# A search's new order for a fused attention and mixing kernel: pieces of its 32-row value products set apart

## The chip, the cores and the metric

The program runs on one core of one Trainium2 chip. The metric is the device time of one execution in microseconds (us), lower is better. The core's engines work side by side, each through its own list of instructions: TensorE (PE in the profile; its weight loads are PEld), VectorE (DVE), ScalarE (ACT), GpSimd (POOL), and SyncE (SP), which here only issues DMAs. They meet at semaphores.

## What is computed

The reference, cut to what matters; there are 8 batches, 8 heads, 576 positions and 64 numbers per head, all in fp32:

```python
scores = matmul(q, k.T) / sqrt(64)
scores = where(scores >= scores.max(-1) - tau, scores, -1e9)
attn = exp(scores - scores.max(-1));  attn = attn / (attn.sum(-1) + 1e-9)
x = matmul(attn, v)                                # heads side by side: (8, 576, 512)
theta = x @ w_theta
y = w_tok_r @ (x * cos(theta)) + w_tok_i @ (x * sin(theta))
u = x + y
out = u + maximum(u @ w_ch, 0)
```

## The kernel before

The 64 heads are worked in 32 pairs. For each pair five *units* of score products run on TensorE (line 761, 12 or 6 matmuls each). VectorE takes the scores out of PSUM with their largest value (782), ScalarE makes the exponentials (815), VectorE masks and sums them (822). Then the weights of the attention are turned round, in one of two ways. In 12 pairs TensorE does it with transposes (855) and the value product runs with 64 rows (920). In the other 20 pairs VectorE turns blocks of 32 by 32 (837, 839), and the value product runs with 32 rows and 64 columns of the array, eight such products side by side (891): 144 fp32 matmuls of 144 columns in the program, which become 288 passes in the trace, each with a weight load of its own. These are the *small value products* of this text. All of a pair's value product goes into PSUM banks 0 to 3, and ScalarE copies it out at its end (904, 907). After every fourth pair a batch is complete and its mixture follows: angles and the last product on TensorE (1021), sines on ScalarE (1117 to 1124), products with x on GpSimd or VectorE (1139), transposes of z (1164) and the token product (1209). The mixture of one batch is spread among the attention of the next.

A pair's small value products are cut into three *pieces*, each one step of the plan with 48 matmuls of the program:

```python
parts = AT["parts"]                                # 3
for i in range(parts):
    c0, c1 = 18 * i // parts, 18 * (i + 1) // parts
    pe((c1 - c0) * w / 600 + 0.05, lambda c0=c0, c1=c1: products(c0, c1),
       key + A("vs", n) * i, (a, v), (ps,), 32 * (c1 - c0), mode="w", hold=[x])
```

The code first makes a list of 4617 steps, each for one engine, with what it reads and writes. Nothing is scheduled when the kernel is built: the table `ORDER` holds, as differences, the numbers of the steps in the order in which they are emitted, and the table `PLACES` holds the buffer of each class that a step's tile takes. Both come from an offline search over a plan with costs; the search is not part of the file. `Plan.run` walks the table:

```python
n = 0
for word in ORDER.split():
    step, times = (word + "*1").split("*")[:2]
    for _ in range(int(times)):
        n += int(step)
        self.ops[n].fn()
```

Each engine gets its own steps in that order and works them strictly one after another.

Of the kernel before, what the change touches and what calls it, by code (L numbers as in the profile page):

```python
# [142 lines left out]
    "176 3 -9 3 75 -71 -176 177 2 -153 144 10 -9 79 -251 183 -169 160 -134 135 -122 131 146 -145 2 -1 3 8 -9 -186 "  # L143
    "188 59 -246 195 -5 -189 191 4 -8 10 -5 4 11 -19 -187 197 1 -197 22 185 -204 185 -187 205 -197 202 -13 21 27 -2 "
    "-43 8 38 -27 -21 4 -193 211 2 25 -40 17 8 -11 -220 325 -125 8 -206 2 198 -156 164 195 -372 14 127 58 -19 -15 "
    "-164 181 -212 219 26 -239 225 -229 228 -9 -10 -3 -189 301 -74 -20 -4 -9 -168 164 15 23 -229 209 22 -17 27 64 -2 "
    "-98 10 91 -99 51 210 -238 13 -10 26 -42 90 -91 26 -228 220 30 -4 -28 -14 43 -16 10 11 122 -141 18 -21 24 -279 "
    "273 -16 223 -479 280 -3 -19 21 9 -22 15 -278 260 -16 42 -283 258 3 -18 35 6 -40 -2 38 -25 26 -286 394 -113 -270 "
    "290 -300 281 -10 12 -281 258 41 93 -383 232 -240 299 -290 278 -285 312 -28 -276 279 -58 57 -34 140 -104 -49 155 "
    "-385 304 -20 -4 -36 -241 279 102 -79 -16 -288 30 350 -98 24 -1 -16 27 -32 -283 306 1 -16 -289 287 43 -40 173 "  # L150
    "-148 -38 571 -534 -26 43 -326 332 -21 -10 13 8 -321 311 3 12 -304 -21 332 -309 -1 309 5 -3 1 -23 -309 335 7 -53 "
    "30 14 -13 -317 299 -2 44 -41 537 -526 29 -3 -24 -15 -292 306 41 -11 -346 342 -24 -5 -302 445 -424 305 -23 44 "
    "-59 26 133 -119 -1 -326 -10 455 -108 -336 1 336 -3 28 -330 800 -505 -317 -8 333 -345 449 -428 -7 309 -26 153 "
    "-77 -16 -335 429 -438 361 -344 -7 1 362 -355 -16 341 -301 321 -18 -6 -320 -30 348 28 -345 -8 877 -527 -332 -9 "
    "-7 326 -327 9 289 27 52 -55 -312 1 8 316 -2 -331 297 62 -38 55 -16 -26 -318 -6 367 -26 -19 46 -366 349 -321 309 "
    "33 -18 -346 10 344 11 -4 -17 -333 355 -373 19 333 25 -3 1 -367 -6 352 -343 -2 855 -488 -31 40 -53 14 -326 343 "
    "15 -16 -3 -16 -333 350 -330 353 -26 -336 21 339 3 -40 -312 -20 375 119 -148 11 13 4 -372 -1 18 -9 2 317 58 -11 "
    "-373 18 309 -319 332 36 9 -375 30 334 -355 345 425 -386 -17 -366 -9 780 -769 353 -363 329 444 -764 366 399 -381 "
    "-380 28 -40 364 -12 422 -764 3 378 -376 352 535 -533 6 -364 393 -388 437 -83 23 -51 52 27 -43 -13 3 37 372 -355 "
    "-43 -3 30 -389 349 474 -417 -28 338 -356 47 -406 1 9 390 -10 -388 9 705 -327 -377 366 13 -368 -10 872 -168 -693 "  # L160
    "383 -404 22 694 -705 -10 725 -337 -13 22 19 -27 -388 716 -706 2 -10 9 -10 396 -18 -2 -356 359 -377 372 350 -347 "
    "15 -2 -15 -354 367 5 -2 334 -711 10 -2 -10 714 -14 -689 -8 722 -348 327 -309 -382 689 -701 396 -5 -377 711 79 "
    "-100 -315 -376 695 -2 -309 -7 -375 383 4 324 -19 -304 -11 317 -305 312 -311 338 -344 -6 334 -327 -5 22 297 30 "
    "61 -398 298 10 -304 389 -394 2 337 2 55 -384 36 263 -308 344 -343 391 -449 60 1 309 24 -26 34 -5 57 -88 10 -5 "
    "-304 302 149 -448 297 -305 343 -26 -308 332 -335 4 -3 345 -37 -314 317 18 17 5 -16 -331 343 -20 -322 343 -327 "
    "288 43 -330 331 -330 315 -312 -20 349 -6 -322 -20 347 7 -24 20 -333 315 3 -317 -17 350 -303 301 174 -167 -354 3 "
    "350 -352 4 -3 4 356 -50 9 -317 39 291 -327 356 -28 -310 19 -34 331 -301 -14 15 396 -428 10 23 399 -404 8 14 -32 "
    "-19 12 312 -294 340 65 -422 18 91 -100 -8 416 -307 -100 101 -104 323 -319 410 80 -395 252 60 -368 -24 60 215 "
    "-214 -75 16 79 716 -735 246 -245 19 -100 19 63 247 -27 -214 1 238 -306 62 -89 341 -251 -62 9 54 -80 316 -231 "
    "-65 79 -81 68 -85 22 77 -13 -68 19 43 7 260 -321 -6 18 292 -230 -73 -26 87 -67 7 61 721 -706 -81 58 9 -51 -8 17 "  # L170
    "57 -76 11 20 46 -72 73 -77 78 214 -213 1 -69 20 -29 33 26 -29 283 -281 -1 261 -210 -48 49 238 -22 -263 56 243 "
    "-256 214 -200 -9 -49 -24 74 9 -14 -79 13 72 -48 43 14 -92 84 -77 27 59 2 -1 -9 206 -255 60 5 -15 11 5 218 -217 "
    "230 -324 288 37 -20 21 -16 137 -369 234 -197 187 17 -314 111 197 -196 187 -303 319 -314 309 -312 303 21 -320 "
    "105 -33 16 219 -201 -17 -88 89 1 -89 109 198 -217 20 202 -207 -103 109 -63 -47 90 217 5 -220 216 10 2 -272 -46 "
    "319 -2 3 2 -211 184 -294 90 230 7 -32 -293 74 246 -321 322 -245 13 194 44 -209 -28 236 5 -212 1 202 6 1 6 -12 "
    "-214 223 -241 39 -38 244 -194 -21 -28 237 7 1 13 -17 -212 217 -229 242 -258 17 242 -241 221 -220 252 -41 16 "
    "-226 243 10 -244 306 -314 251 -12 -238 317 -338 -9 293 55 -338 287 -277 325 -314 241 -3 29 46 -299 254 -261 244 "
    "3 -239 303 -302 683 -447 3 -238 18 -108 81 1 -19 273 -305 52 243 -235 -7 8 -7 14 1 212 -217 224 -226 244 -243 "
    "24 -22 246 -245 220 21 -237 217 15 13 -244 232 -14 9 18 -244 240 5 -17 -16 34 11 -28 18 -241 207 395 -350 -31 "
    "-220 196 56 -10 -248 9 253 -13 21 -11 1 -13 -246 239 429 -406 -9 -4 -240 241 20 -19 352 -597 254 -6 -244 242 "  # L180
    "-245 264 -6 7 -261 277 -287 265 7 -271 605 -340 -253 276 53 -75 340 -593 296 -17 -278 273 -49 36 36 -49 346 "
    "-592 260 21 15 291 -340 50 -22 -18 54 277 -306 -281 273 381 -397 25 -281 1 273 22 3 257 -554 281 -7 24 -11 16 "
    "252 -256 -19 20 -18 65 -64 18 412 -157 2 -254 -2 258 -276 273 2 5 -278 2 1 19 -13 271 -256 1 254 -269 13 -33 "
    "291 7 -269 -30 37 340 -339 -7 17 325 -86 -248 254 82 -333 258 -251 -9 45 -42 251 80 -59 -271 -53 310 -291 285 "
    "-245 247 -256 398 -386 233 -232 248 -257 10 261 -238 -27 5 17 -27 6 236 -231 17 1 -17 261 -240 238 -241 4 -3 "
    "219 25 -230 -32 33 -11 222 -221 4 -26 265 -27 6 -211 234 -266 26 -22 261 -264 2 275 -4 -272 20 -17 32 280 -60 "
    "22 -20 -232 -21 274 -247 248 -243 -30 35 224 196 -188 -236 -11 290 -50 -7 -254 37 338 -112 -1 7 6 -248 -24 19 "
    "16 -5 231 -213 -49 32 18 218 -101 -141 25 404 -403 137 -162 45 203 -629 368 59 180 -216 207 -191 21 190 -210 5 "
# [1197 lines left out]
```

## Time and profile before

| | |
|---|---|
| Time, median of 3 runs | 952.08 us (949.31 to 953.31) |
| Time of the profiled execution | 950.14 us |
| Its span, first to last instruction | 948.3 us |
| PE busy | 904.9 us (95%) |
| DVE busy | 796.5 us (84%) |
| ACT busy | 634.1 us (67%) |
| POOL busy | 342.8 us (36%) |
| Small value products (L891), PE busy, and idle just before them | 105.9 us, 12.9 us |

The profiled execution is 1.94 us shorter than the median of the runs. Busy time of PE is the union of its matmuls' times; a matmul's end is modelled and overlaps the next one's start, so a short wait of PE can lie unseen inside busy time.

### The profile page before, as it was taken

Reading aid. Unit: us, or ns where it says so; the run is one execution under the profiler, and the core shown is the slowest. Engines: PE = TensorE matmul, PEld = TensorE weight load, DVE = VectorE, ACT = ScalarE, POOL = GpSimd, SP = SyncE. Lnnn points to the kernel's source line nnn. Section 1 sums busy time; section 2 is a strip of 40 time slices with the busy share of each in tenths; the row PEclk is TensorE's granted clock in tenths of the full one; section 3 lists DMA queues with packets and bytes.
Section 4 is the critical chain, followed back from the end, with each engine's and each line's share of the span. In section 5 each row is a group of like instructions: output and inputs, shape, how many; then the busy total and the mean of one; then the engine's idle time right before and its main releaser. Section 6 shows DMA issues by size and latency. Waiting matters only on the chain.

```text
span 948.3 us, 30033 instructions
## 1 busy us (share of the span) xinstructions
PE 904.9 (95%) x12532; PEld 801.8 (85%) x12532; DVE 796.5 (84%) x1838; ACT 634.1 (67%) x1296; POOL 342.8 (36%) x390
## 2 busy tenths in 40 slices
PE   6889999999999999999899999999999999999998
PEld 5667788898898889888798988898898988899798
DVE  7999899979988988889798897879998798986342
ACT  7899997458945777467764767548784578635650
POOL 2234453125624345234432533432442353404110
PEclk9999999999999999999999999999999999999999
DMA  6366253435322353325403453044533153222322
GB/s 219 125 195 199 85 184 125 142 123 192 122 86 92 116 178 120 127 78 179 147 37 104 136 192 112 4 172 122 192 99 112 55 196 123 70 97 98 114 70 73
DMA packets 59288, 118.80 MB, mean 125 GB/s; under 512 B 19441, under 2 KB 28561, under 8 KB 56593
## 3 DMA queue, kind: packets, MB, share of 16 engines
q1 hardware_dynamic: 59008, 116.89, 37.2%
q8 instruction: 98, 1.61, 0.7%
q14 instruction: 38, 0.30, 0.1%
q10 hardware_dynamic: 144, 0.00, 0.0%
HBM read 103.09 MB, written 13.78 MB: 123 GB/s over the span
## 4 chain that ended last, share of the span: by engine, by line
PE 60%; DVE 22%; ACT 10%; issue 5%; POOL 2%; DMA 0%; SPq 0%; DVEq 0%; ACTq 0%; POOLq 0%
PE banks_ps__66 L1209 19%; PE banks_ps__66 L1021 12%; PE banks_ps__66 L761 10%; PE banks_ps__66 L891 9%; DVE sc L782 6%; DVE s L822 6%; PE banks_ps__66 L855 4%; DVE a L837 4%; PE banks_ps__66 L1164 3%; PE banks_ps__66 L920 2%; ACT s L815 2%; POOL z L1139 1%; DVE xl L539 1%; DVE z L1089 1%; ACT L1117 1%
## 5 line engine op out<-in xcount | busy, mean ns | idle before, releaser
L815 ACT ACTIVATE s<-sc,nm 128x576 f32<-128x576 f32 x288 | 219.5, 777 | 73.0 <-DVE sc L782 57.3
L822 DVE SCALAR_TENSOR_TENSOR s<-sc,nm,s 128x576 f32<-128x576 f32 x288 | 249.7, 888 | 14.9 <-ACT s L815 7.9
L782 DVE TENSOR_SCALAR_CACHE_REDUCE sc<-banks_ps__66 128x576 f32<-128x576 f32 x261 | 188.3, 744 | 23.0 <-PE banks_ps__66 L761 21.7
L761 PE MATMUL banks_ps__66<-k,q 64*128 64x288 f32 (+1 forms) x1728 | 173.9, 313 | 12.9 <-DVE sc L782 7.9
L1021 PE MATMUL banks_ps__66<-xh,wm 128*128 128x288 f32 x1024 | 170.9, 304 | 2.2 <-issue 1.6
L761 PEld LDWEIGHTS banks_ps__66<-k,q 64*128 64x128 f32 (+1 forms) x1728 | 137.9, 189 | 39.8 <-issue 15.2
L1209 PE MATMUL banks_ps__66<-wt_h,zh 128*128 128x288 f32 x576 | 159.1, 303 | 1.3 <-ACT zh L1170 0.4
L1209 PE MATMUL banks_ps__66<-wt_l,zh 128*128 128x288 f32 x576 | 158.0, 299 | 0.0
L1021 PEld LDWEIGHTS banks_ps__66<-xh,wm 128*128 128x128 f32 x1024 | 144.8, 190 | 9.5 <-issue 6.2
L1139 POOL TENSOR_TENSOR z<-z,xT 128x288 f32<-128x288 f32 x112 | 98.7, 914 | 128.6 <-ACT z L1120 118.0
L837 DVE STREAM_TRANSPOSE a<-s 128x576 f32<-128x576 f32 x160 | 117.4, 757 | 20.6 <-PE banks_ps__66 L891 18.6
L539 POOL TENSOR_TENSOR xl<-xT,xh 128x288 fp32r<-128x288 f32 x78 | 75.3, 987 | 141.8 <-ACT xh L982 120.5
L891 PE MATMUL banks_ps__66<-a,v 32*64 32x144 f32 x5760 | 105.9, 286 | 12.9 <-issue 11.0
L1209 PEld LDWEIGHTS banks_ps__66<-wt_h,zh 128*128 128x128 f32 x576 | 106.8, 188 | 7.0 <-issue 4.1
L891 PEld LDWEIGHTS banks_ps__66<-a,v 32*64 32x64 f32 x5760 | 91.5, 130 | 23.5 <-issue 18.9
L1209 PEld LDWEIGHTS banks_ps__66<-wt_l,zh 128*128 128x128 f32 x576 | 107.3, 188 | 2.0 <-issue 1.9
L539 POOL TENSOR_TENSOR k<-rawk,k 128x288 fp32r<-128x288 f32 x62 | 57.9, 942 | 113.7 <-ACT k L722 78.1
L1209 PE MATMUL banks_ps__66<-wt_h,zl 128*128 128x288 f32 x576 | 98.7, 299 | 0.0
L539 POOL TENSOR_TENSOR q<-rawq,q 128x320 fp32r<-128x320 f32 x56 | 57.8, 1045 | 111.8 <-ACT q L708 111.8
L1021 PE MATMUL banks_ps__66<-xl,wm 128*128 128x288 f32 x512 | 92.6, 301 | 0.9 <-DVE xl L539 0.6
L1209 PEld LDWEIGHTS banks_ps__66<-wt_h,zl 128*128 128x128 f32 x576 | 82.8, 188 | 1.4 <-issue 1.2
L855 PE MATMUL banks_ps__66<-ident,s 128*128 128x128 f32 (+1 forms) x492 | 74.8, 284 | 3.1 <-DVE s L822 2.1
(84 smaller groups left out, 1275.0 us busy)
## 6 DMA issues: line engine op xcount, KB each, us to landing
wm<-wm_dram SPq DMA_DIRECT2D x64, 512.0 KB
v<-in_vp_dram SPq DMA_DIRECT2D x20, 1152.0 KB
rawq<-in_qT_dram SPq DMA_DIRECT2D x31, 320.0 KB
rawk<-in_kT_dram SPq DMA_DIRECT2D x31, 288.0 KB
out_dram<-xT SPq DMA_DIRECT2D x31, 288.0 KB
rb<-sums_dram SPq DMA_DIRECT2D x64, 128.0 KB
v<-in_vp_dram SPq DMA_DIRECT2D x12, 576.0 KB
z<-in_w_tok_dram SPq DMA_DIRECT2D x9, 576.0 KB
```

Of the source, the lines that this page charges most:

```text
L539: eng.tensor_tensor(out=out()[:, c0:c1], in0=in0()[:, c0:c1], in1=in1()[:, c0:c1], op=ALU.subtract)
L761: nc.tensor.matmul(ps()[:, 2 * j + h, :HS], q[a]()[r, i * P : (i + 1) * P], k[c]()[r, h * HS : (h + 1) * HS], start=(x == 0), stop=(x == 2),)
L782: lambda j=j, sc=sc, scaled=scaled: nc.vector.tensor_scalar(out=sc().rearrange("p (a b) -> p a b", a=2), in0=ps()[:, 2 * j : 2 * j + 2, :H ...
L815: lambda j=j, sc=sc, weights=weights: nc.scalar.activation(out=weights(), in_=keys(sc()), func=AF.Exp, bias=nm()[:, j : j + 1], scale=-1.0),
L822: lambda j=j, sc=sc, total=total, weights=weights: nc.vector.scalar_tensor_tensor(out=weights(), in0=keys(sc()), scalar=nm()[:, 2 + j : 3 ...
L837: nc.vector.transpose(out=a()[:, :, j, 32 * i : 32 * i + 32], in_=src.rearrange("p (c q) -> p c q", q=32))
L855: nc.tensor.transpose(out=tp()[: k1 - k0, c * P : (c + 1) * P], in_=flat()[:, k0:k1], identity=ident)
L891: nc.tensor.matmul(ps()[64 * h : 64 * h + 64, b, :w], v()[r, c, h, :], a()[r, c, h, :], start=(c == 0), stop=(c == 17))
L1021: nc.tensor.matmul(ps[h]()[:, :HS], wm()[:, a, c, :], parts[c][bb]()[:, h * HS : (h + 1) * HS], start=first and n == 0, stop=final and n = ...
L1139: eng.tensor_tensor(out=zi, in0=zi, in1=x[m]()[:, c0:c1], op=ALU.mult)
L1164: nc.tensor.transpose(out=tp()[:, i * P : (i + 1) * P], in_=z()[:, c : c + P], identity=ident)
L1209: nc.tensor.matmul(ps()[:, :HS], zz[c][lo]()[:, zz[c][2]], w[:, c, hs], start=(q + n == 0), stop=(q + n == len(work) - 1),)
```

## The change

Only `ORDER` differs: other numbers, one line more. The list of steps, their code, the buffers of `PLACES` and all cost numbers are the same, so every line below the table moves from L to L+1 (L891 is L892 in the new file), and every instruction runs the same work on the same tiles. On VectorE 701 of 1225 steps stand at another place in its list, on ScalarE 650 of 1170, on GpSimd 252 of 384 and among the DMA issues 193 of 292; the mean step there moves by 1.1 to 1.3 places and the furthest by 16. A line or two of the table:

```diff
 ORDER = (
-    "176 3 -9 3 75 -71 -176 177 2 -153 144 10 -9 79 -251 183 -169 160 -134 135 -122 131 146 -145 2 -1 3 8 -9 -186 "
...
+    "13 9 5 -4 16 -11 7 -3 4 -3 4 3 -2 3 2 -1 2 "
 )
```

The clearest difference is on TensorE. In the order before, 17 of the 20 pairs have two of their three pieces directly behind each other, 96 matmuls in a row (a *doubled piece*). In the rows below L1021 is the mixture's products of channels, L1164 the transposes of z, L946 a transpose of the row sums, L855 the transposes of attention weights and L1209 the token product; `xh` and `xl` are the two parts of an operand, `zh` and `zl` too. On TensorE before, all three pieces of the pair that stands at 457 to 468 us of the trace:

```order
L891 MATMUL banks_ps__66<-a,v 64x144 x48
L1021 MATMUL banks_ps__66<-xl,wm 128x288 x4
L1021 MATMUL banks_ps__66<-xh,wm 128x288 x8
L891 MATMUL banks_ps__66<-a,v 64x144 x96
L1164 MATMUL banks_ps__66<-ident,z 128x128 x4
```

The same pair after:

```order
L892 MATMUL banks_ps__66<-a,v 64x144 x48
L1022 MATMUL banks_ps__66<-xh,wm 128x288 x8
L1022 MATMUL banks_ps__66<-xl,wm 128x288 x4
L892 MATMUL banks_ps__66<-a,v 64x144 x48
L1022 MATMUL banks_ps__66<-xl,wm 128x288 x4
L892 MATMUL banks_ps__66<-a,v 64x144 x48
L1165 MATMUL banks_ps__66<-ident,z 128x128 x8
```

Four matmuls of L1021 that stood elsewhere now part the second piece from the third.

On TensorE before, the last two pieces of the last such pair (855 us):

```order
L1209 MATMUL banks_ps__66<-wt_h,zl_12838 128x288
L891 MATMUL banks_ps__66<-a,v 64x144 x96
L855 MATMUL banks_ps__66<-ident,s_13096 128x128
L1209 MATMUL banks_ps__66<-wt_h,zl_12838 128x288 x3
```

After:

```order
L1210 MATMUL banks_ps__66<-wt_h,zl_12835 128x288
L892 MATMUL banks_ps__66<-a,v 64x144 x48
L856 MATMUL banks_ps__66<-ident,s_13109 128x128
L892 MATMUL banks_ps__66<-a,v 64x144 x48
L856 MATMUL banks_ps__66<-ident,s_13002 128x128 x4
```

Here a single transpose went in between the two. One doubled piece is left, in the pair at 386 us; on TensorE after:

```order
L1165 MATMUL banks_ps__66<-ident,z 128x128 x4
L892 MATMUL banks_ps__66<-a,v 64x144 x96
L1210 MATMUL banks_ps__66<-wt_h,zh_5565 128x288
```

The first two pieces of this pair stayed together, with four transposes ahead of them instead of a row of L1209.

Counted over the whole list of TensorE, the two nearest pieces of a pair stand this many matmuls of other work apart after: 0 in one pair, 1 in two, 3 or 4 in five, 5 to 7 in seven, 9 to 21 in five. Before it was 0 in 17 pairs, and 12, 17 and 21 in the other three. From the first piece to the last of a pair there are 20.6 matmuls of other work on average, before 20.9. Ahead of each of the 160 score products (L761) the same steps of TensorE stand as before, but for six at most.

## Rows read from the trace of the kernel before

**Rows 1.** The page: span, busy time, the span in 40 slices.

```profile
span 948.3 us, 30033 instructions
PE 904.9 (95%) x12532; PEld 801.8 (85%) x12532; DVE 796.5 (84%) x1838; ACT 634.1 (67%) x1296; POOL 342.8 (36%) x390
...
PE   6889999999999999999899999999999999999998
...
DVE  7999899979988988889798897879998798986342
```

**Rows 2.** Windows by stage: us, then busy time of each engine (instructions), clock.

```profile
0.00:144.00 144.00, 125.94 (x1121) 98.00 (x1122) 132.42 (x327) 128.75 (x280) 53.28 (x74) 0.98 0.53 169
144.00:864.00 720.00, 699.61 (x10780) 628.06 (x10778) 628.29 (x1438) 469.61 (x945) 279.46 (x304) 1.00 0.36 120
864.00:949.00 85.00, 79.37 (x637) 75.78 (x633) 35.74 (x75) 35.78 (x73) 10.08 (x13) 0.99 0.28 95
```

**Rows 3.** PE's waits from 144 to 864 us: for whom, us, times, longest.

```profile
PE banks_ps__66 L891 <- issue: 11.0, 9, 2.0
PE banks_ps__66 L1021 <- issue: 1.6, 1, 1.6
PE banks_ps__66 L891 <- DVE a L839: 1.4, 4, 0.5
PE banks_ps__66 L1164 <- POOL z L1139: 1.4, 3, 0.9
PE banks_ps__66 L761 <- DVE sc L782: 1.0, 3, 0.4
```

**Rows 4.** PE's timeline from 460 us: start, length, count, [idle before, releaser].

```profile
460.88 1.01 PE L891 MATMUL banks_ps__66<-a,v 32*64 32x144 f32 x45
462.82 2.25 PE L891 MATMUL banks_ps__66<-a,v 32*64 32x144 f32 x128 [0.93 <-issue]
467.10 0.70 PE L891 MATMUL banks_ps__66<-a,v 32*64 32x144 f32 x19 [2.02 <-issue]
```

**Rows 5.** The page: DMA queue, packets, MB, share of 16 engines.

```profile
q8 instruction: 98, 1.61, 0.7%
```

**Rows 6.** PE's timeline: three pieces of one pair that stand apart.

```profile
348.90 1.78 PE L891 MATMUL banks_ps__66<-a,v 32*64 32x144 f32 x96 [0.16 <-DVE a L839]
350.61 0.80 PE L1021 MATMUL banks_ps__66<-xh,wm 128*128 128x288 f32 x4
351.25 0.69 PE L1021 MATMUL banks_ps__66<-xl,wm 128*128 128x288 f32 x4
351.77 0.70 PE L1021 MATMUL banks_ps__66<-xh,wm 128*128 128x288 f32 x4
352.31 0.69 PE L1021 MATMUL banks_ps__66<-xl,wm 128*128 128x288 f32 x4
352.93 1.78 PE L891 MATMUL banks_ps__66<-a,v 32*64 32x144 f32 x96
...
356.33 1.78 PE L891 MATMUL banks_ps__66<-a,v 32*64 32x144 f32 x96
```

**Rows 7.** PE's timeline: a doubled piece without a stop.

```profile
164.49 3.25 PE L891 MATMUL banks_ps__66<-a,v 32*64 32x144 f32 x192
167.66 0.66 PE L1164 MATMUL banks_ps__66<-ident,z 128*128 128x128 f32 x4
```

**Rows 8.** Who waited for the small value products: us, times.

```profile
  ACT xT L904: 50.4, 16
  DVE a L837: 18.6, 6
```

**Rows 9.** PE's timeline: a transpose of z that waited ahead of a piece.

```profile
246.55 0.55 PE L1164 MATMUL banks_ps__66<-ident,z 128*128 128x128 f32 x3 [0.85 <-POOL z L1139]
247.03 3.25 PE L891 MATMUL banks_ps__66<-a,v 32*64 32x144 f32 x192
```

322 rows, old and new, of the table ORDER are left out of this document.

## The prediction

> **What bounds the kernel now.** I read the page's busy time first, then the windows by stage, then who waits in the stage that is longest. TensorE is busy for 95% of the span and in no slice after the first below eight tenths [rows 1]. The windows show three stages [rows 2]. Up to 144 us VectorE is busy for 132.4 us and ScalarE for 128.8, TensorE for 125.9: there TensorE waits for the others. From 144 to 864 us TensorE is busy for 699.6 of 720 us, VectorE for 628.3 (87%), ScalarE for 469.6, at the full clock: TensorE is the bound, and 20.4 us of it are idle. The tail from 864 us is nearly all TensorE again. So the question is what TensorE's idle time between 144 and 864 us consists of. The list of its waits answers it [rows 3]: 11.0 us in nine waits stand inside the small value products (L891) and 1.6 us in one stands right behind a doubled piece, all put down to "issue", that is to nothing that the profile sees another engine or a DMA of the program doing. Each of the waits for a named engine comes to 1.4 us or less in total.
>
> The timeline shows what these ten stops are [rows 4]. A doubled piece of 192 passes starts at 460.88 us. It runs 45 passes, stands, runs 128 passes, stands again, and ends with 19. Each pass has a weight load of its own, so 128 passes are 256 instructions. The page has a DMA queue for instructions, with 98 packets and 1.61 MB [rows 5], 16.4 KB each; TensorE's 12532 matmuls and as many weight loads [rows 1], divided by 98, are 256 per packet. So TensorE's instructions come in blocks of 256, and a doubled piece, which uses up 384 in 3.2 us, runs out of them. I take the stops to be late instructions; the rows make it likely and don't prove it.
>
> [...]
>
> **The change part by part.** Only the order differs. I sum against the profiled execution, 950.1 us with a span of 948.3; the median of the runs is 1.9 us longer, which I add at the end.
>
> *What a stop costs now.* The idle time that a row shows begins at the modelled end of the last pass, 0.28 us after its start (the first stop of [rows 4]: 45 passes at the pace of the 128 that follow are started by 461.6, the next one starts at 462.82, which is 1.2 us for 0.93 shown). So the ten stops cost 12.6 + 10 × 0.28 = 15.4 us, 1.54 each on average. With 17 doubled pieces that is 0.59 stops per piece; some have none [rows 7].
>
> *What parting two pieces costs.* In [rows 6] a piece starts at 348.90 and the next at 352.93, 4.03 us later, with 16 matmuls of L1021 in between. Eight of these take 1.06 us where nothing else borders on them (351.25 to 352.31), 0.13 each, so 16 are 2.12 and the lone piece costs 1.91. It comes in three steps: 1.71 from its start to the next instruction's, 0.11 more in the first four matmuls behind it (0.64 against 0.53), 0.09 more in the four ahead of it (0.62 against 0.53). A doubled piece takes 3.17 [rows 7], with the same two borders 3.37. Two lone ones are 3.82: each parting costs 0.45 us of TensorE's time, a little less where a transpose borders on it. Sixteen pairs are parted: 16 × 0.43 = 6.9 us, all on the engine that is the bound. Nothing covers this.
>
> *What is left of the stops.* Instructions are fetched ahead, so other work between two pieces gives the fetch time: n matmuls take n × 0.13 us, where the same number of small passes takes n × 0.017, and the parting itself adds 0.43. A stop of 1.54 us thus shrinks by 0.43 + 0.116 n. By the counts of the order, that leaves 1.54 us in the pair that is still doubled, 0.99 in each of the two with one matmul between, 0.7 on average in the five with three or four, 0.3 to 0.5 in the seven with five to seven, and nothing to speak of from nine on. The sum over the 20 pairs is 9.5 us; times 0.59, 5.6 us. The three pairs that stood 12 or more apart before had no stop [rows 6], which agrees. So 15.4 - 5.6 = 9.8 us are won. The bounds: all 15.4, if a small gap suffices; or, if every stop were as long as the longest (from 462.82 to 467.10 is 4.28 us for 256 instructions, whose own starts take 2.1, so 2.2), the same sum gives 12.2 left and 3.2 won.
>
> *All other moves.* The work of a pair from first piece to last is the same (20.6 other matmuls against 20.9), so PSUM banks 0 to 3 and the one buffer `a` are held as long as before. The score products, which feed VectorE, have the same steps ahead of them but for six at most, and the other engines' steps move by about one place. In the first 144 us, where VectorE and ScalarE set the time, their work ahead of each score product is the same, so I cost that stage at nothing. The DMA issues on SP move by 1.3 places on average; no wait of TensorE from 144 us on is put down to a DMA [rows 3]. What the moves can win elsewhere is bounded by TensorE's other waits in the main stage: 20.4 idle less the 12.6 is 7.8 us. What they can lose I bound by the same amount. I take 0. VectorE has 92 us of slack in the 720, so a stop that goes away should count in full; where it does not, the cover is [rows 8], ScalarE and VectorE waiting for a value product's end.
>
> *Sum.* 6.9 - 9.8 = -2.9 us: 947.2 for the profiled execution, 949.2 us on the scale of the median, -0.3%. About 0.5%, or 4.8 us, is what a measurement of this kernel can tell from no change, so the likeliest outcome is a small gain that hardly shows.
>
> **The rivals.**
>
> *The stops vanish altogether.* Even a few matmuls between are enough, because the next block is asked for some way ahead of the end of the present one. For it: eight of the 17 doubled pieces had no stop although they ran 384 instructions in one go. Against it: one matmul between, as in two pairs, is hardly a pause. Then 15.4 are won and 6.9 paid: 952.1 - 8.5 = 943.6 us.
>
> *A late value product holds up VectorE (slower).* The buffer `a` is freed, and the banks are copied out, only when the third piece ends. Parting makes that end later by 0.43 us and by what is pushed in between. VectorE waited for it six times, 3.1 us each [rows 8]. As long as VectorE makes up for that before the next score products need it, nothing is lost; if the added 0.6 us or so reaches the score products of all 20 pairs, 12 us come on top of the -2.9: 961 us. Against it: the window from first to last piece holds no more work than before, and each stop that shrinks ends it earlier. The same in small would be transposes of z between the pieces that find z late, at 0.85 us of idle time as in [rows 9]; the pieces wait behind them.
>
> *The stops are not late instructions, or the parting does not touch them.* They would then stay with the pieces wherever these stand, and only the price comes: 952.1 + 6.9 = 959.0 us. Against it is [rows 4].
>
> *The new order takes other waits away.* Half of the 7.8 us on top of the forecast: 945.3 us. For it: a search made the order. Against: hardly anything else has moved far.
>
> **How the numbers follow.** The forecast has 0.45, the vanishing stops 0.27, the later value product 0.12, the price alone 0.08, the other waits 0.08. Each has a spread of some 4 us around its time, from the bounds of the stops and of the other moves. The limits are 947.3 and 956.8 us. Faster by over 0.5%: 0.09 of the forecast, 0.22 of the second, 0.06 of the last, together 0.37. Slower: 0.02 of the forecast, 0.10 and 0.06 of the two slow rivals, 0.18. Within: 0.45. The range of 8 in 10 goes from 943 (just beyond the vanishing stops) to 956 (the sum with the longest stop everywhere, 952.1 + 6.9 - 3.2).
>
> **What would show it.** In the profile after, TensorE's busy time rises by some 4 to 7 us from the partings, and the small value products' waits for issue fall from 11.0 us to 2 to 5 us, left mainly in the pair at 386 us and in those with one matmul between. A piece with work of nine matmuls or more on both sides stops nowhere. If waits of 1 us or more still stand in pieces set well apart, the cause is not the one I take. If the time falls by 8 us or more, the stops are gone and I asked too much of the gap. If it rises, rows of VectorE's score reads (L783) or of the weights' transposes waiting for L892 must have grown.

## The result, and the profile after

The changed kernel took 935.79 us (934.86 to 936.75) against 951.71 us of the kernel before in the same comparison: a ratio of 0.985, with a 95% interval from 0.983 to 0.988. That is 15.9 us less, where 2.9 were forecast, and below the range of 943 to 956. Run again beside the variants below it took 936.95 us against 950.08, a ratio of 0.986 (0.983 to 0.989).

Of the 15.9 us the two profiled executions show 13.4 (950.14 and 936.75 us). The other 2.5 come from where each stands to its own median: before 1.6 under 951.71, after 1.0 over 935.79.

The page after: span, busy time and TensorE's slices, the instruction queue, and the group of the small value products (its busy time, the mean ns of one, the idle time just ahead).

```profile
span 935.0 us, 30039 instructions
PE 905.9 (97%) x12532; PEld 803.9 (86%) x12532; DVE 795.2 (85%) x1838; ACT 633.5 (68%) x1296; POOL 336.4 (36%) x390
...
PE   6889999999999999999999999999999999999998
...
q8 instruction: 98, 1.61, 0.7%
...
L892 PE MATMUL banks_ps__66<-a,v 32*64 32x144 f32 x5760 | 109.4, 287 | 4.4 <-issue 2.4
```

Beside [rows 1] TensorE's busy time hardly changed (904.9 to 905.9 us), and its idle time fell from 43.4 to 29.1 us. Busy time must not be read as work here: the small value products alone show 3.5 us more of it (105.9 to 109.4), so other groups show less, with the same instructions on the same tiles. Short waits lie unseen inside the modelled busy time.

TensorE's waits after, in the main stage (for whom, us, times, longest), to be read beside [rows 3]:

```profile
PE banks_ps__66 L892 <- issue: 2.4, 3, 0.8
PE banks_ps__66 L1165 <- POOL z L1140: 1.5, 2, 0.9
PE banks_ps__66 L892 <- DVE a L840: 1.3, 2, 1.0
PE banks_ps__66 L947 <- DVE rows L943: 0.7, 1, 0.7
...
PE banks_ps__66 L1165 <- issue: 0.3, 1, 0.3
```

The waits for issue fell from 12.6 us in ten to 2.7 in four. All waits for named engines together fell from 7.3 us to 5.5 (from 144 to 850 us in both traces); the large loss at one named wait that my slow rival needed is not there.

TensorE's timeline after, at the pair of [rows 4]:

```profile
453.25 1.78 PE L892 MATMUL banks_ps__66<-a,v 32*64 32x144 f32 x96
...
456.74 1.78 PE L892 MATMUL banks_ps__66<-a,v 32*64 32x144 f32 x96
458.45 0.80 PE L1022 MATMUL banks_ps__66<-xl,wm 128*128 128x288 f32 x4
459.18 1.48 PE L892 MATMUL banks_ps__66<-a,v 32*64 32x144 f32 x75
461.46 0.71 PE L892 MATMUL banks_ps__66<-a,v 32*64 32x144 f32 x21 [0.80 <-issue]
```

Two stops of 0.93 and 2.02 us have become one of 0.80, in the third piece, which has only four matmuls ahead of it. Another of 0.81 us stands in a third piece at 567 us, again with four matmuls ahead. The third large one that is left is different. It stands in the third piece of the pair at 382 us, whose first two are still doubled, and that piece has nine matmuls of the token product ahead of it and six of them and a unit of score products behind:

```profile
386.45 0.96 PE L892 MATMUL banks_ps__66<-a,v 32*64 32x144 f32 x38
388.15 1.24 PE L892 MATMUL banks_ps__66<-a,v 32*64 32x144 f32 x58 [0.75 <-issue]
```

To see in which stage the time went, I take one score product at each end of the main stage: the first of the seventh pair and the first of the last. TensorE's timeline before:

```profile
138.09 0.80 PE L761 MATMUL banks_ps__66<-k,q 64*128 64x288 f32 x8
...
844.54 0.92 PE L761 MATMUL banks_ps__66<-k,q 64*128 64x288 f32 x10
```

and after:

```profile
135.76 1.00 PE L762 MATMUL banks_ps__66<-k,q 64*128 64x288 f32 x7
...
830.69 0.80 PE L762 MATMUL banks_ps__66<-k,q 64*128 64x288 f32 x7
```

So 2.3 us were won up to the seventh pair, 11.5 in the main stage (706.45 to 694.93), and 0.5 lost behind it (948.3 - 844.54 against 935.0 - 830.69): 13.3, the difference of the spans.

Counted from each matmul's start to the next one's, where no wait can hide, the main stage's 11.5 us lie in these groups: 6.3 less at the small value products (109.7 to 103.4), 2.8 less at the products of channels, 1.9 less at the token product (three matmuls fewer lie in the stage), 1.0 less at the transposes of the attention weights, and 1.0 more at the transposes of z; all others change by 0.3 us or less.

### The profile page after: what moved, and what is told of

The parts are those of the page before. It is cut to its first block, busy times and chain, and to the rows that moved or that the text cites. A ratio compares the mean times of both kernels' runs of the same rounds, so it can differ in the third digit from the quotient of the medians.

```text
span 935.0 us, 30039 instructions
## 1 busy us (share of the span) xinstructions
PE 905.9 (97%) x12532; PEld 803.9 (86%) x12532; DVE 795.2 (85%) x1838; ACT 633.5 (68%) x1296; POOL 336.4 (36%) x390
## 4 chain that ended last, share of the span: by engine, by line
PE 72%; DVE 14%; ACT 7%; issue 3%; POOL 2%; DMA 1%; SPq 0%; DVEq 0%; ACTq 0%; POOLq 0%
PE banks_ps__66 L1210 24%; PE banks_ps__66 L1022 14%; PE banks_ps__66 L762 12%; PE banks_ps__66 L892 10%; DVE sc L783 5%; PE banks_ps__66 L856 4%; DVE s L823 4%; PE banks_ps__66 L1165 4%; PE banks_ps__66 L921 3%; DVE a L838 2%; ACT s L816 1%; ACT a L862 1%; POOL z L1140 1%; PE banks_ps__66 L642 1%; DVE xl L540 1%
## 5 line engine op out<-in xcount | busy, mean ns | idle before, releaser
L783 DVE TENSOR_SCALAR_CACHE_REDUCE sc<-banks_ps__66 128x576 f32<-128x576 f32 x261 | 189.2, 745 | 20.9 <-PE banks_ps__66 L762 19.2
L1140 POOL TENSOR_TENSOR z<-z,xT 128x288 f32<-128x288 f32 x112 | 95.7, 887 | 121.7 <-ACT z L1121 121.5
L838 DVE STREAM_TRANSPOSE a<-s 128x576 f32<-128x576 f32 x160 | 117.9, 759 | 16.0 <-PE banks_ps__66 L892 14.1
L540 POOL TENSOR_TENSOR xl<-xT,xh 128x288 fp32r<-128x288 f32 x78 | 73.3, 958 | 128.2 <-ACT xh L983 115.4
L892 PE MATMUL banks_ps__66<-a,v 32*64 32x144 f32 x5760 | 109.4, 287 | 4.4 <-issue 2.4
L892 PEld LDWEIGHTS banks_ps__66<-a,v 32*64 32x64 f32 x5760 | 91.5, 130 | 16.6 <-issue 11.5
```

What stands on the lines that cost most here:

```text
L540: eng.tensor_tensor(out=out()[:, c0:c1], in0=in0()[:, c0:c1], in1=in1()[:, c0:c1], op=ALU.subtract)
L783: lambda j=j, sc=sc, scaled=scaled: nc.vector.tensor_scalar(out=sc().rearrange("p (a b) -> p a b", a=2), in0=ps()[:, 2 * j : 2 * j + 2, :H ...
L838: nc.vector.transpose(out=a()[:, :, j, 32 * i : 32 * i + 32], in_=src.rearrange("p (c q) -> p c q", q=32))
L892: nc.tensor.matmul(ps()[64 * h : 64 * h + 64, b, :w], v()[r, c, h, :], a()[r, c, h, :], start=(c == 0), stop=(c == 17))
L1140: eng.tensor_tensor(out=zi, in0=zi, in1=x[m]()[:, c0:c1], op=ALU.mult)
```

## The experiments

Times are medians; every ratio is to the kernel before, run on the same chip, with its 95% interval. A diff shows one place; `x48` counts matmuls of the program, and lines have the numbers of the kernel before. The kernels are called by short names: *after* is the changed kernel.

**Parting alone.** In *parted* only the middle piece moves, in 17 pairs, to the middle of the pair's other work; everything else is the order before.

```diff
-L891 MATMUL banks_ps__66<-a,v 64x144 x96
-L1164 MATMUL banks_ps__66<-ident,z 128x128 x4
-L1209 MATMUL banks_ps__66<-wt_l,zh 128x288
...
+L891 MATMUL banks_ps__66<-a,v 64x144 x48
+L1164 MATMUL banks_ps__66<-ident,z 128x128 x4
...
+L891 MATMUL banks_ps__66<-a,v 64x144 x48
```

> The order before, with one kind of move alone: in each of the 17 pairs whose value product has two pieces side by side, the middle piece is put in the middle of the work that stands between the first and the last piece (4 to 17 matmuls on either side). Nothing else moves on any engine. Theory A (the stops are late instructions and parting cures them, at a price of about 0.3 us per parting): waits for issue in L891 fall from 11.0 to under 3 us, about 12 us won and 5 paid, 944 to 946 us. Theory B (the new order's other moves carry most of the 16 us): 948 to 952 us here. Theory C (the prediction's price of 0.43 us per parting): about 947 us, TensorE busy 6 us longer.

It took 949.76 us, ratio 0.9992 (0.9973 to 1.0011): no change. The stops are gone all the same. TensorE's busy time on the page, and its waits in the main stage:

```profile
PE 913.8 (96%) x12532; PEld 803.8 (85%) x12532; DVE 793.9 (84%) x1838; ACT 633.2 (67%) x1296; POOL 338.2 (36%) x390
```

```profile
PE banks_ps__66 L897 <- issue: 3.0, 2, 2.4
PE banks_ps__66 L952 <- DVE rows L948: 2.1, 3, 1.2
```

The waits for issue fell from 12.6 to 3.4 us (the 3.0 and two of 0.2), and busy time rose by 8.9. That fits the terms of my sum (9.8 won, 6.9 paid) without measuring them one by one, since busy time hides waits; the waits for named engines rose from 7.3 to 8.7 us. The interval of the result reaches from 2.6 us less to 1.0 more, so the 2.9 less that I forecast lie just outside. Parting by itself takes most of the stops away and is worth next to nothing.

**The other moves alone.** In *rejoined* the order of after stays, and the middle pieces go back beside the neighbour that they had before.

```diff
-L1164 MATMUL banks_ps__66<-ident,z 128x128 x4
-L891 MATMUL banks_ps__66<-a,v 64x144 x48
-L1164 MATMUL banks_ps__66<-ident,z 128x128 x5
-L891 MATMUL banks_ps__66<-a,v 64x144 x48
+L1164 MATMUL banks_ps__66<-ident,z 128x128 x9
+L891 MATMUL banks_ps__66<-a,v 64x144 x96
```

> The order after, with the middle piece put back beside the neighbour that it has in the order before, in 17 pairs; nothing else moves. Theory A: the stops come back (about 11 us) and the price goes (about 5): 942 to 944 us, that is half of the gain is kept by the other moves. Theory B': everything hangs on the parting, the rest is worth nothing: 950 to 952 us.

946.94 us, ratio 0.9960 (0.9946 to 0.9973), 4.3 us less than before and between my two ranges, with stops of 9.3 us back. So the two halves of the change are worth some 1 and 4 us apart and 13 to 16 together. One place where the moves alone fall short is the transposes of the attention weights, by line on TensorE (busy, mean ns, idle ahead): before, then rejoined, then after.

```profile
L855 PE MATMUL banks_ps__66<-ident,s 128*128 128x128 f32 (+1 forms) x492 | 74.8, 284 | 3.1 <-DVE s L822 2.1 <-ACT wt_l L647 0.7 <-ACT q L708 0.2
```

```profile
L862 PE MATMUL banks_ps__66<-ident,s 128*128 128x128 f32 (+1 forms) x492 | 76.1, 284 | 9.0 <-DVE s L829 3.8 <-ACT wt_l L654 1.9 <-DVE xT L1228 1.7
```

```profile
L856 PE MATMUL banks_ps__66<-ident,s 128*128 128x128 f32 (+1 forms) x492 | 76.4, 284 | 6.0 <-DVE s L823 2.6 <-ACT wt_l L648 2.2 <-ACT xT L932 0.5
```

With the pieces put together TensorE waits 3.0 us more there than in after. The waits of before and after lie ahead of the seventh pair, and rejoined has 3.2 us in the main stage, where the others have 0.1 or less. I take it that TensorE comes to these transposes too early, so that part of what joining saves is given back; no run shows that by itself.

**Are the stops late instructions?** In *shift* the order before stays, behind 192 instructions more on TensorE, so that the blocks of 256 end elsewhere.

```diff
     nc.vector.tensor_scalar(out=minus, in0=ident, scalar1=-1.0, scalar2=None, op0=ALU.mult)
+    for _ in range(96):
+        nc.tensor.matmul(psum[:16, 7, :16], minus[:, :16], minus[:, :16], start=True, stop=True)
```

> The order before, unchanged, behind 96 tiny matmuls (16 by 16, results unused) at the very start, where TensorE waits for its first operands up to 4.8 us: 192 instructions more ahead of everything. All doubled pieces stay doubled. Theory A (instructions come in blocks of 256, and a stop falls where the end of the blocks at hand lies inside a doubled piece): the ends move by 192 instructions against the pieces, the eight doubled pieces that stopped run through, and by counting only the one around 855 us has such an end in it; stops shrink from 15 us to 2 to 5, 940 to 944 us. Rival (the stops belong to the pieces or to their data): the same pieces stop, 950 to 954 us.

943.23 us, ratio 0.9928 (0.9905 to 0.9950), from a change of 96 useless matmuls. The stops went to other pieces. One and the same doubled piece on TensorE's timeline, before:

```profile
496.65 2.97 PE L891 MATMUL banks_ps__66<-a,v 32*64 32x144 f32 x172
500.56 0.71 PE L891 MATMUL banks_ps__66<-a,v 32*64 32x144 f32 x20 [0.94 <-issue]
```

and with the shift:

```profile
498.88 3.25 PE L894 MATMUL banks_ps__66<-a,v 32*64 32x144 f32 x192
```

The piece, its data and its neighbours are the same; only its place in the count of instructions moved, and the stop is gone. I numbered TensorE's instructions in each trace from the start, weight loads and waits on semaphores included, and took all places inside a small value product where 0.9 us or more pass from one pass's start to the next one's. There are 70 over the twenty traces of this study, and all stand at the same place of the count, behind the 193rd instruction of a group of 256. With the packets' landings in the last section, that settles late instructions as the cause. More stops were left than expected, seven against one:

```profile
PE banks_ps__66 L894 <- issue: 7.1, 7, 1.4
```

**Whose list carries the rest?** Each engine's list can be exchanged by itself as long as no engine then waits for one that waits for it. That rules out TensorE's or VectorE's list of after with the other's of before (argued from the waits; no run shows it). In *pe-dve* these two are those of after and the other three those of before; in the next three kernels after has one list of before.

```diff
 TensorE, VectorE: list of after
-ScalarE, GpSimd, SyncE: list of after
+ScalarE, GpSimd, SyncE: list of before
```

> TensorE's and VectorE's lists of the order after, with the lists of ScalarE, GpSimd and the DMA issues of the order before. If what the other moves won (about 5 us of TensorE's other waits) lies on TensorE and VectorE: 935 to 938 us, as after. If it lies on the other three: 939 to 942 us.

963.27 us, ratio 1.0135 (1.0117 to 1.0153): 12 us slower than before, which none of my theories allowed. Next, one at a time; at the start of ScalarE's list the exchange reads:

```diff
-L708 CAST q<-rawq 128x640
 L815 ACTIVATE s<-sc,nm 128x9x64 x2
 L585 ACTIVATE xl<-wm 128x512
-L815 ACTIVATE s<-sc,nm 128x9x64
+L708 CAST q<-rawq 128x640
+L815 ACTIVATE s<-sc,nm 128x9x64
```

> The changed kernel with ScalarE's list alone put back as before; TensorE's pieces stay parted. What it tells: which list carries the 27 us between the changed kernel (936) and the kernel with the lists of ScalarE, GpSimd and SyncE put back (963). If ScalarE's list carries the fit, because it holds the copies out of PSUM, the exponentials and the sines, this costs at least half of it: 949 to 963 us, with waits of TensorE for scores (VectorE) and for xh. If GpSimd's list carries it, as the waits for z (4.6 us) and xl (2.1 us) in that kernel suggest: 936 to 941 us. If the loss was spread evenly or needs several lists together: 941 to 949 us.

> The changed kernel with GpSimd's list alone put back as before. If GpSimd's list carries the fit: 949 to 963 us, with TensorE's waits for z back at 4 us or more between 144 and 864 us (1.5 us in the changed kernel). If ScalarE's or SyncE's list carries it: 936 to 941 us. If the loss is spread: 941 to 949 us.

> The changed kernel with SyncE's list of DMA issues alone put back as before. No wait of TensorE from 144 us on was put down to a DMA, so by the reading that the engines' own lists carry the fit this costs little: 936 to 940 us. If the order of the DMA issues carries it (loads and stores that keep buffers of the other engines): 949 to 963 us, and waits of ScalarE, GpSimd or VectorE for DMAs must grow by several us.

ScalarE's list alone: 962.81 us, ratio 1.0120 (1.0103 to 1.0136), the whole loss. GpSimd's: 945.95, ratio 0.9943 (0.9923 to 0.9962). SyncE's: 946.81, ratio 0.9950 (0.9931 to 0.9969). My bet on GpSimd fell, and so did the one that DMA issues cost nothing. TensorE's waits with ScalarE's old list:

```profile
PE banks_ps__66 L1168 <- POOL z L1143: 3.8, 6, 0.9
PE banks_ps__66 L765 <- DVE sc L786: 2.7, 6, 1.0
...
PE banks_ps__66 L1213 <- DVE zl L1193: 2.3, 1, 2.3
```

None of these names ScalarE (3.5 of the 16.9 us of named waits in that stage do), and yet only its list changed. VectorE's waits show one way in which it comes about: masking the scores waits 11.5 us for ScalarE's negated maximum, 5.7 in after.

```profile
DVE s L826 <- ACT nm L797: 11.5, 15, 2.0
```

```profile
DVE s L823 <- ACT nm L794: 5.7, 6, 1.7
```

With SyncE's old list about half of the loss is early: the seventh pair's first score product comes 4.5 us later than in after, of 9.5 us in the two spans. The window from 40 to 60 us (length, then busy time of PE, PEld, DVE, ACT and POOL, and clock, DMA share and GB/s at the end) of that kernel, one of its waits there, and the window of after:

```profile
40.00:60.00 20.00, 14.89 (x154) 11.04 (x152) 16.24 (x44) 16.01 (x34) 2.39 (x4) 0.98 0.51 159
```

```profile
ACT rawq L708 <- DMA rawq<-in_qT_dram: 3.8, 1, 3.8
```

```profile
40.00:60.00 20.00, 17.83 (x181) 14.11 (x180) 19.83 (x54) 18.78 (x42) 2.39 (x4) 1.00 0.49 145
```

A load of q is issued later in that list, ScalarE waits for it, and TensorE and VectorE lose some 3 us each.

**Better, or only matched?** The reverse exchange, in the order before:

```diff
 TensorE, VectorE, ScalarE: list of before
-GpSimd: list of before
+GpSimd: list of after
```

> The order before with GpSimd's list alone taken from the new order. Putting the old list of GpSimd into the new order cost 9 to 10 us. If the new list is better in itself, it makes the old order faster: 940 to 948 us. If the lists of a plan only have to match each other, it costs here as well: 955 to 962 us. If it is neither: 949 to 953 us.

> The order before with SyncE's list of DMA issues alone taken from the new order. Putting the old list into the new order cost 10 us, much of it in the first 144 us. If the new list is better in itself: 940 to 948 us. If the lists only have to match each other: 955 to 962 us. If it is neither: 949 to 953 us.

> The old order with its pieces set apart in the middle (950 us with the old lists), and the lists of GpSimd and SyncE of the new order. If these two lists are what lets parting pay: 936 to 944 us. If VectorE's and ScalarE's lists have to move with TensorE's, too: 949 to 952 us, or more, 952 to 965 us, if the lists only have to match.

With GpSimd's new list 952.65 us, ratio 1.0025 (1.0003 to 1.0047); with SyncE's 952.82, ratio 1.0010 (0.9992 to 1.0029); the parted order with both 949.03, ratio 0.9974 (0.9957 to 0.9991). So these lists are no better in themselves, nor do they let parting pay in the old order. Out of place they cost some 2 us at most in the old order and 9 to 11 in the new one. I take it that the new order has less slack to hide them; no run measures that.

**Does it matter where the piece stands?** In *recentred* the order of after has its middle pieces at the middle of the pair's work, by the rule of parted. In *gaps* the order before has 14 middle pieces as far from the same neighbour as in after. The edit of recentred, at one pair:

```diff
 L1209 MATMUL banks_ps__66<-wt_l,zh 128x288
+L891 MATMUL banks_ps__66<-a,v 64x144 x48
 L1164 MATMUL banks_ps__66<-ident,z 128x128
-L891 MATMUL banks_ps__66<-a,v 64x144 x48
 L1209 MATMUL banks_ps__66<-wt_h,zh 128x288
```

> The changed kernel with the middle piece of 17 pairs moved to the middle of its pair's work, by the same rule by which the pieces of the old order were set apart with no gain; all else of the new order stays. Four to eleven matmuls then stand on either side, so fewer instruction stops are left than in the changed kernel. If the new order of the other steps is what lets parting pay, and the place of a piece within its pair matters little: 932 to 938 us. If the gain lies in where exactly the new order put each piece, as filler while other inputs were not ready, then the waits of TensorE for other engines come back: 941 to 948 us.

> The order before with the middle piece of 14 pairs set as many matmuls away from the same neighbour as it has in the changed kernel (three pairs stay doubled for want of a step that small); all other steps as before. If the place of the pieces makes the gain: 938 to 943 us. If the other steps have to move with them: 946 to 951 us, like the old order with its pieces parted in the middle (950).

Recentred: 938.43 us, ratio 0.9876 (0.9851 to 0.9902), 1.5 us more than after. Gaps: 951.29, ratio 1.0014 (0.9999 to 1.0029). Pieces set apart by either rule pay 12 to 16 us in the new order (recentred and after) and 1 us or nothing in the old one (parted and gaps). So where exactly a piece stands matters little, and the order of the steps around it decides whether parting pays.

TensorE's waits for named engines show part of how the two belong together. From 144 to 850 us they come to 7.3 us in before, 8.7 in parted and 10.6 in gaps; and to 9.4 in rejoined, 6.7 in recentred and 5.5 in after. Pieces set apart add waits in the old order and take them away in the new one.

**The gain by parts of the span.** In *new-then-parted* all engines follow after up to the 19th pair (some 480 us in the trace, not the 530 of the expectation) and parted from there; *parted-then-new* is the reverse.

```diff
 steps ahead of the first score product of pair 19: order of after
-steps from there: order of after
+steps from there: order of parted
```

> The new order for all engines up to the first score product of the 19th of the 32 pairs (some 530 us), and from there the old order with its pieces parted in the middle (the kernel of 950 us). The changed kernel is at 937, so 13 us lie between the two. If the gain of the new order is local, the sum of many small waits all along: it keeps the part that was won by 530 us, by the times at which the pairs' score products begin some 8 us, so 941 to 944 us. If the order of a whole plan only works as one, the gain is lost at the seam or behind it: 947 us or more.

> The reverse: the old order with its pieces parted in the middle up to the first score product of the 19th pair, from there the new order. If the gain is local and adds up: the part won behind 530 us, some 5 us, so 943 to 947 us, and the two gains of this pair of kernels sum to 11 to 15 us. If the order only works as one: 948 us or more.

941.34 us, ratio 0.9915 (0.9896 to 0.9933), and 943.43, ratio 0.9929 (0.9909 to 0.9948). Parted has the ratio 0.9992 to its own runs of before, so these are 0.8% and 0.6% below it, some 7.3 and 6.0 us or 13.3 together, where after is 12.5 to 13.2 below parted. The gain is local, and its halves add up. It is no single event, and the plan need not be one piece.

**Is there something faster?** *Last pair* parts the doubled piece that is left at 382 us. Two kernels put the 96 tiny matmuls ahead of after and ahead of last pair.

```diff
-L891 MATMUL banks_ps__66<-a,v 64x144 x96
+L891 MATMUL banks_ps__66<-a,v 64x144 x48
 L1209 MATMUL banks_ps__66<-wt_h,zh 128x288
 L1209 MATMUL banks_ps__66<-wt_l,zh 128x288
 L1209 MATMUL banks_ps__66<-wt_h,zh 128x288
+L891 MATMUL banks_ps__66<-a,v 64x144 x48
```

> The changed kernel with its one doubled piece that is left, in the pair at 383 us, parted too (3 and 6 matmuls apart). Its one shown stop of 1.03 us would shrink, and the parting costs some 0.4 us: 0.3 to 1 us faster than the changed kernel at best, 935 to 936 us, the same within what can be measured. A rise by 2 us or more would say that the fit of the order to its pieces is that close.

> The changed kernel itself, for a comparison on one chip with the three variants. It had 935.8 us with a mean granted clock of 0.998 in all four runs; the kernel before and the variants ran mostly at 0.993 to 0.998, and within one kernel 0.001 of it went with 0.66 us. If the granted clock of the first 80 us differs by chance from run to run, runs at 0.995 show up here, of 937 to 939 us: 935 to 938 us in all. If the new order itself keeps the clock up: 936 us again, all at 0.998.

> The changed kernel behind 96 tiny matmuls, 192 instructions, at the start, so that the ends of the blocks of 256 instructions fall elsewhere. By late instructions, counted from the starts of the instructions: about 2 to 4 us of stops go (of the 4.4 us shown inside the small value products there remain 1 to 2), one long stop appears near 776 us; 932 to 936 us. If the changed kernel's gain came from where the blocks' ends happen to fall in its order, and not from parting, the shift takes it away: 941 to 947 us. If the remaining stops have nothing to do with the blocks: 936 to 938 us (the 96 tiny matmuls lie in the loading at the start).

> The changed kernel with its last doubled piece parted, behind 96 tiny matmuls (192 instructions). The changed kernel behind the same 96 had one stop of 3.5 us in that doubled piece and took 940.2 us; with the piece parted that stop should nearly go. By late instructions: 2 to 3 us less than that, 936 to 938 us, about the changed kernel itself or a little below it. If the long stop stays or moves to another place: 939 to 941 us.

Last pair took 936.62 us, after beside it 936.95: the same. After shifted took 940.15, ratio 0.9865 (0.9845 to 0.9885), and last pair shifted 939.86, ratio 0.9876 (0.9846 to 0.9906): slower than after, where I had expected them a little faster. (Of the 4.4 us named in the expectation only 2.4 were waits for issue.) The shift that took 7 to 8 us off the order before puts a block's end into the third piece of the pair at 382 us. TensorE's timeline of that piece, after shifted and then last pair shifted:

```profile
390.84 1.45 PE L895 MATMUL banks_ps__66<-a,v 32*64 32x144 f32 x70
395.75 0.73 PE L895 MATMUL banks_ps__66<-a,v 32*64 32x144 f32 x26 [3.46 <-issue]
```

```profile
388.32 1.45 PE L901 MATMUL banks_ps__66<-a,v 32*64 32x144 f32 x70
392.09 0.73 PE L901 MATMUL banks_ps__66<-a,v 32*64 32x144 f32 x26 [2.32 <-issue]
```

In both kernels the stop stands in a lone piece, not in the doubled one that the expectation names: in after shifted it has nine matmuls ahead, in last pair shifted six, with three more between the first two pieces. The stop went from 3.46 to 2.32 us, not away. No version beat after.

**How much of the gain is where the blocks end?** Read side by side, the two shifted kernels answer it for one shift. After shifted, at 940.15 us, already lies nearer to the second range of its expectation (941 to 947, the gain came from where the blocks' ends fall) than to the first (932 to 936). Behind the same 96 matmuls the old order has the ratio 0.9928 and the new one 0.9865. There the change is worth 0.6%, some 6 us by the ratios and 3 by the medians (943.23 and 940.15, from two sets), and not 13 to 16. The same score products as above, with the shift, in the old order and then in the new one:

```profile
139.45 0.80 PE L764 MATMUL banks_ps__66<-k,q 64*128 64x288 f32 x8
...
837.04 0.79 PE L764 MATMUL banks_ps__66<-k,q 64*128 64x288 f32 x8
```

```profile
137.59 0.96 PE L765 MATMUL banks_ps__66<-k,q 64*128 64x288 f32 x7
...
835.76 0.80 PE L765 MATMUL banks_ps__66<-k,q 64*128 64x288 f32 x8
```

The main stage takes 697.59 us in the one and 698.17 in the other. TensorE's waits for issue in it are 6.2 us in seven in the old order and 5.0 in four in the new one; with 0.28 us more for each, as in the prediction, parting wins only some 2 us on stops there. More than half of the measured gain therefore hangs on where the blocks happened to end in the two kernels as they were compared; other shifts were not run.

## Why the prediction was wrong

- **What bounds the kernel** was read rightly: TensorE, and its waits for issue are instructions that come late. The shift shows it. What I had not weighed is how few of the crossings cost anything. In before TensorE came past the 193rd instruction of a group of 256 at 84 places between 144 and 864 us. At 67 of them the packet that a stop there waits for (last section) had landed more than 2 us earlier, and over all 84 it had landed 5.6 us earlier in the median. Ten crossings, nine inside the small value products and one right behind, cost some 1.54 us each by my estimate.
- **The price of parting** held. After has four matmuls between two pieces at 458.45 us, and the next piece starts 0.73 us later: 0.53 for the four, 0.11 and 0.09 for the two borders of [rows 6]. With 1.71 for the piece itself that is the 0.45 that I took per parting.
- **The stops that are left** came close in sum: 5.6 us were forecast, and the four that show come to 2.7 + 4 x 0.28 = 3.8. Two stand behind short gaps, as I had it. So 11.6 us were won, not 9.8. But the size is partly luck: behind the 96 matmuls the same parting wins some 2 us on stops, against the same 6.9 paid. And my rule for the gap is wrong. The third piece of the pair at 382 us has work of nine matmuls and more on both sides, and it stops: for 0.75 us in this profile, for 1.32 in the second profile of after, and for 3.46 in after shifted. My sign "stops nowhere" failed; by the sign next to it (waits of 1 us or more in pieces set well apart) late instructions would be the wrong cause, and the shift shows that they are the right one. Behind some stops the granted clock fell as well (to 0.50 for 3.41 us behind the one of 1.64 us in before), a cost that I had missed; more below.
- **"All other moves ... I take 0"** is the step that failed. In the main stage 11.5 us went: 11.6 won on stops less 6.9 paid is 4.7, so 6.8 come from elsewhere, and 2.3 more from the first 138 us, which I had costed at nothing. About 1.7 of the 6.8 are clock. The same sum for the two shifted kernels gives 4.3 from elsewhere in the main stage (2.0 won less 6.9 paid would be 4.9 more, and 0.6 more were measured), or 6.0 without the 1.7 us of clock that after shifted lost there. So some 5 to 6 us from the other moves show at both places of the blocks' ends. My reason for 0 was that steps had moved by one place on average. Exchanging single lists shows how little that says: single lists out of place cost some 2 us at most in the old order and up to 27 in the new one (962.81 against 935.79).
- **The bound of 7.8 us** on these moves was too narrow. I took it from TensorE's idle time in one stage of one profile. It left out waits inside modelled busy time, the first stage, and the clock. Of the waits that it did count, the named ones, only 1.8 us went (7.3 to 5.5).
- **The sum itself** failed in adding. Parting alone gave about 1 us and the other moves alone 4, which as independent terms would make 6, within 3 of my forecast; together they gave 13 to 16.
- **The rivals.** The slow one did not come: VectorE's waits for the value product's end fell from 18.6 us in six [rows 8] to 14.1 in eight, and ScalarE's from 50.4 to 47.4. In the rows after:

```profile
ACT xT L905 <- PE banks_ps__66 L892: 47.4, 17, 9.2
DVE a L838 <- PE banks_ps__66 L892: 14.1, 8, 4.2
```

The vanishing stops came in part. The rival that came true is the one I gave 0.08, that the new order takes other waits away, and with twice its size (6.8 and 2.3 us, clock included, for 3.9). My last test line, "if the time falls by 8 us or more, the stops are gone", would have named the wrong rival.

What stays open: why TensorE's other waits shrink only when the pieces stand apart *and* all engines follow the new lists. ScalarE's list put back alone loses the whole gain and more; TensorE's and VectorE's can't be exchanged one by one, so no run here splits these two. The rejoined kernel bears on it only in part, since putting pieces together also moves everything between them.

## What to carry to other kernels

In an order written step by step, cost a change of order by the waits of all engines and not by how far steps move: a list whose steps stood one place off on average cost 9 to 27 us in the new order here and some 2 at most in the old one. When a profile shows waits for nothing inside dense runs of tiny instructions, put some dummy instructions ahead; if the waits move, the instructions come late, and where the blocks happen to end is luck (here worth 0.7% of the old order). Compare two orders with more than one such shift before you call one of them faster. Test two parts of a change apart and together before adding their prices.

## What the runs showed of the hardware

**A block of instructions lands later where the program's own DMAs keep the DMA engines busy.** Windows of before around the stop of 2.02 us at 465 us (the last columns are the clock, the DMA share and GB/s):

```profile
457.00:462.00 5.00, 4.51 (x153) 3.90 (x154) 4.75 (x12) 4.97 (x8) 0.96 (x1) 1.00 0.81 271
...
463.00:467.00 4.00, 2.08 (x128) 1.82 (x121) 0.00 (x0) 1.07 (x1) 4.00 (x7) 1.00 0.19 46
```

The 16 DMA engines were 81% busy just ahead. I took six traces (before, after, parted and the three shifted), some 530 packets of the instruction queue in the stages from 144 us on, and for each the time from TensorE's start of an instruction about 300 ahead of the block's to the packet's landing (that is where the spread of this time is smallest). Its median is 2.2 us where the DMA engines were under a tenth busy in between, 2.7 from there to a half, and 3.6 above a half, with one in ten over 6.1. The packet itself takes 1.0 us in all three, so the time goes by ahead of it; what it waits for there was not shown. A stop ended 1.3 to 1.6 us after a landing. So my single stop length, shrunk by the gap, could not tell that a piece with four matmuls ahead would still stop for 2.4 us (parted, where the DMA share was 0.98 from 460 to 463 us).

**Behind some stops the granted clock fell.** Windows of before behind the stop of 1.64 us that ends at 577.98 us, and TensorE's timeline there; then the same twelve score products in after, whose stop there is 0.81 us:

```profile
574.00:578.00 4.00, 2.36 (x155) 2.09 (x139) 0.00 (x0) 1.91 (x3) 4.00 (x7) 1.00 0.24 62
578.00:582.00 4.00, 4.00 (x33) 3.36 (x34) 2.20 (x4) 2.93 (x9) 3.01 (x4) 0.67 0.66 211
```

```profile
579.41 1.81 PE L761 MATMUL banks_ps__66<-k,q 64*128 64x288 f32 x12
```

```profile
571.56 1.07 PE L762 MATMUL banks_ps__66<-k,q 64*128 64x288 f32 x12
```

The granted clock was 0.50 for 3.41 us from 579.39 us on, and the score products took 1.81 us for 1.07. From 570 to 600 us before had 0.94 of the clock, 1.7 us of it missing; after had 1.00 there. In the parted kernel the clock fell likewise behind its stop of 2.4 us (a mean of 0.57 from 466 to 470 us), in after shifted behind the one of 3.5 (0.58 from 396 to 399). It is not so behind every stop: of the ten in before only this one was followed by a fall, and the one of 2.02 us at 467 us was not (1.00 from 467 to 470 us). The nine executions of after had a mean clock of 0.998 to 1.000, those of before mostly 0.993 to 0.996; within one kernel 0.001 went with about 0.6 us (a fit over the executions of all kernels). With means of 0.998 and 0.995 that makes some 2 us of the gain that go with the clock, an estimate. In the first 80 us the dips stand elsewhere from trace to trace (before had 0.91 of the clock from 0 to 20 us and from 20 to 40, after 0.91 from 60 to 80), and the runs of before alone lie between 0.989 and 1.000, so how much of that the order earns stays open.
